# GpSimd's gain product one unit later behind the next reciprocal, and 64x64 blocks for half of the attention values

## The chip, the core and the metric

One core of a Trainium2 chip runs the whole program. The metric is the device time of one execution in microseconds (us); the time of a kernel is the median of its runs. The core has five engines with a queue of instructions each: PE (TensorE, matrix products; PEld is its loading of stationary operands), DVE (VectorE), ACT (ScalarE), POOL (GpSimd) and SP (SyncE, which here only issues transfers). Each engine works through its queue in order; engines wait for each other through semaphores. Transfers issued by SP and by POOL lie in separate queues and share 16 DMA engines.

## What is computed

```python
kv  = einsum('bhsd,bhse->bhde', k, v)            # 8 batches, 8 heads, 576 positions, 64 wide
o   = einsum('bhsd,bhde->bhse', q, kv)
x   = o / sqrt(mean(o*o, -1) + 1e-6) * g_norm    # then (batch*position, head*64): 4608 x 512
# mixture of experts on x
do  = x @ w_skip > 0
e   = argmax(x @ w_gate);  p = softmax(x @ w_gate)[e]
out = x;  out[do] += p * (relu(x @ w1[e]) @ w2[e])   # 8 experts, 512 -> 1024 -> 512
```

All data are fp32. There is no softmax in the attention, so that k^T v is formed once for each head, as a 64x64 matrix.

## The kernel before

**Two phases.** Up to about 130 us the attention runs, in 36 units; behind it the experts run one after the other (layers at lines 983, 994 and 1062). x is not kept on the chip: each finished piece is stored to `out`, and the experts gather their rows from there.

**Units.** A unit (`units`, line 390) is 256 positions of one batch (two rows for each of 128 partitions) and four of the eight heads (`u`). A batch b has four units with i = 0, 1; after batches 3 and 7 come two units with i = None, which hold the ninth part of the positions of four batches. Units 0 to 15 are batches 0 to 3, 16 and 17 the first i = None pair, 18 to 33 batches 4 to 7, 34 and 35 the last pair.

**Steps.** The order of all instructions is written out by hand (`tc.manual_schedule()`, line 138), in the loop at line 823. Step n issues:

1. PE: `turn(n+1)`, the transposes of q for the next unit (L421), copied out by ACT (L424);
2. ACT: `root(n-1)`, the square root (L486);
3. PE: `values(n)`, the products of q with k^T v (L457, or L465 where i is None) into one bank pair of PSUM; two such tiles (`o_ps`) take turns, and from unit 28 on (`THIRD`) every third unit uses `sum_ps` instead. ACT squares the result (L471);
4. DVE: `norm(n-1)`, reciprocal (L493) and the product xl = o times reciprocal (L496), which frees the PSUM tile;
5. DVE: `squares(n)`, the sum of squares (L479);
6. PE: the parts of k^T v for a later batch that fall in this step (`jobs(n, "pe")`): `state` three times (L350, in 64x64 blocks), `state_t` (L364), `state_m` (L373), `state_s` (L382), from six steps ahead of the batch's first unit;
7. POOL: `finish(n-1)`: sums of the gate logits lp and lg (L513, and for u = 1 also L517, L521), then the product of xl and g_norm into xb (L531), and after the last unit of a batch the store of half of xb (L552 or L546);
8. DVE: some two to four small operations of the expert choice ("gating"), if a group of units is complete: streams start at steps 12 and 22 (`ends`), and the last group is done after the attention (`choose(LAST)`, line 1310);
9. SP: `jobs(n, "end")`: loads of q, k and v (L115) and the other half of the store (L553 or L547), which is put at the end of step n+1.

In `values`, lines 456 to 461, a unit with a real i takes four products with 128x128 stationary q and 146 columns of a block-diagonal k^T v (two 64x64 heads and zeros beside them); a unit with i = None takes sixteen products of 64x64 blocks with 73 columns (lines 462 to 469), because its four quarters belong to four batches.

**Buffers.** xl has four buffers, xb (one for each batch) two, so the first product of batch b waits until both store halves of batch b-2 have landed. k and v have three buffers, q two.

**What follows the second gating stream.** Its DVE operations rank the experts (`rank_experts`, L667 to L705, steps 24 to 26). L695 writes the order of the experts; SP reads it (L709) and issues the two loads of the first expert's weights, 2 MB each (L309, L312), ahead of the SP half of batch 5's store. `early` (L742 to L763) then computes the first 128 rows, and POOL gathers them (L763).

**After the attention** PE transposes those rows (L960), does part of layer 1 (L983), then the rank of the last group (`rank(LAST)`, L596), the rest of layer 1, and from the row tables made on DVE (L720 to L729) POOL gathers the remaining rows (L950).

## Time and profile before

| | |
|---|---|
| median of 3 runs | 404.38 us (403.63 to 410.05) |
| the profiled execution | 406.39 us, span 404.6 us, mean granted PE clock 0.954 |
| busy share of the span | PE 91%, PEld 79%, DVE 63%, ACT 36%, POOL 31% |
| values L457, 128x128 by 146 | 240 records, mean 298 ns |
| product L531 | 32 (and 4 for i = None), mean 1199 ns |
| xl L496 / sum of squares L479 | 33 and 3, mean 767 ns / 36, mean 678 ns |
| first step / last xl / first transposes of expert rows | 20 us / 130.6 us / 129.4 us |

A line of a timeline has the start in us, the duration in us, the engine, the line of the code, the operation and its operands (what is written before the arrow, what is read after it), the shape and a count of merged records; in brackets the idle time ahead of it and what ended it. An fp32 product of PE has two records of each kind, so "x8" is four products and "x32" sixteen. In the chain of waits a line has start, duration, and what the program's end waited for in that time. In the windows table a row is a stretch with the busy time of each engine, the clock that PE was granted (1.00 is full), the share of the DMA engines in use and GB/s.

### The profile page before, as it was taken

The numbers are of one execution on the slowest core, as the hardware profiler recorded it, in microseconds if no ns is written. First come the engines' busy times: TensorE is split into PE (matmuls) and PEld (weight loads), VectorE is DVE, ScalarE is ACT, GpSimd is POOL, SyncE is SP. The second block draws the span as 40 slices with busy tenths as digits, with TensorE's granted clock in tenths as the row PEclk, the third lists the DMA queues.
The fourth block names the chain that finished last, engine by engine and source line by source line (L and its number), as shares of the span: only waits on it lengthen the run. The fifth ranks groups of instructions, "written<-read, shape, count | busy, mean of one in ns | idle before, by whom it ended". The sixth has DMA issues, their size and how long they took to land.

```text
span 404.6 us, 9627 instructions
## 1 busy us (share of the span) xinstructions
PE 369.5 (91%) x3849; PEld 320.9 (79%) x3849; DVE 253.8 (63%) x623; ACT 144.6 (36%) x384; POOL 125.0 (31%) x197
## 2 busy tenths in 40 slices
PE   6889999899964988999999999989989999999992
PEld 3678987788863948759978987968978988988982
DVE  3233568599977762457674665846765866868821
ACT  1365786566644212203401430520430340431410
POOL 7024576565567333113103302201231211112001
PEclk9589999899968899999999999989999999999998
DMA  8999999996595892427334551670752743710001
GB/s 297 394 390 389 336 363 375 291 346 182 158 396 159 234 365 75 156 106 231 108 160 129 205 211 58 227 256 3 259 194 80 259 146 119 259 54 27 28 2 48
DMA packets 31287, 81.70 MB, mean 202 GB/s; under 512 B 1850, under 2 KB 1858, under 8 KB 31236
## 3 DMA queue, kind: packets, MB, share of 16 engines
q1 hardware_dynamic: 26688, 66.59, 47.0%
q0 software_dynamic: 4528, 14.41, 10.9%
q8 instruction: 32, 0.52, 0.5%
q14 instruction: 19, 0.16, 0.1%
q10 hardware_dynamic: 20, 0.02, 0.0%
HBM read 66.80 MB, written 14.48 MB: 201 GB/s over the span
## 4 chain that ended last, share of the span: by engine, by line
PE 50%; DMA 17%; issue 15%; DVE 10%; POOL 3%; ACT 3%; DVEq 0%; POOLq 0%; ACTq 0%
PE bank L1062 22%; DMA out_dram<-xg,rows 7%; PE bank L994 7%; PE bank L983 5%; DMA out_dram<-xb 4%; PE o_ps L457 4%; DMA xg<-out_dram,src 3%; DVE xl L496 3%; PE sum_ps L350 3%; DMA xg<-out_dram,asrc 2%; PE q_ps L421 2%; PE bank L960 1%; DVE rs L479 1%; PE g_ps L364 1%; POOL out_dram L1204 1%
## 5 line engine op out<-in xcount | busy, mean ns | idle before, releaser
L1072 ACT COPY p<-bank 128x128 f32<-128x128 f32 (+6 forms) x70 | 20.8, 297 | 106.7 <-PE bank L1062 92.6
L1062 PE MATMUL bank<-xt,w 128*128 128x128 f32 (+5 forms) x336 | 55.4, 288 | 0.0
L1066 DVE TENSOR_TENSOR bank<-bank,p 128x128 f32<-128x128 f32 (+6 forms) x70 | 23.6, 337 | 41.6 <-PE bank L1062 40.7
L1062 PEld LDWEIGHTS bank<-xt,w 128*128 128x128 f32 x336 | 47.0, 190 | 1.9 <-DVE bank L1066 1.4
L457 PE MATMUL o_ps<-kvd,qT 128*128 128x146 f32 x240 | 37.0, 298 | 3.9 <-DVE xl L496 1.8
L1204 POOL DMA_INDIRECT out_dram<-xg,rows x16 | 16.2, 1012 | 76.2 <-DVE xg L1201 74.7
L531 POOL TENSOR_TENSOR xb<-xl,g_b 128x512 f32<-128x512 f32 x32 | 38.4, 1199 | 1.3 <-DMA out_dram<-xb 1.3
L457 PEld LDWEIGHTS o_ps<-kvd,qT 128*128 128x128 f32 x240 | 32.8, 195 | 5.8 <-DVE xl L496 3.0
L1062 PE MATMUL bank<-xs,s 128*128 128x128 f32 (+5 forms) x224 | 36.7, 289 | 0.0
L994 PE MATMUL bank<-w,ht 128*32 128x128 f32 (+2 forms) x448 | 36.6, 322 | 0.0
L1204 POOL DMA_INDIRECT out_dram<-xg,arows x8 | 9.0, 1130 | 81.0 <-DVE xg L1201 80.7
L950 POOL DMA_INDIRECT xg<-out_dram,src x15 | 16.2, 1082 | 53.4 <-DMA out_dram<-xg,rows 27.9
L479 DVE TENSOR_REDUCE rs<-sq 128x8 f32<-128x512 f32 x36 | 24.4, 678 | 12.4 <-ACT sq L471 12.2
L1062 PEld LDWEIGHTS bank<-xs,s 128*128 128x128 f32 x224 | 31.1, 190 | 1.0 <-ACT p L1072 0.8
L994 PEld LDWEIGHTS bank<-w,ht 128*32 128x32 f32 (+2 forms) x448 | 20.4, 121 | 13.6 <-issue 10.9
L1062 PE MATMUL bank<-w,ht 128*128 128x256 f32 x112 | 28.7, 401 | 0.1
L496 DVE TENSOR_TENSOR xl<-o_ps,rs 128x584 f32<-128x584 f32 x33 | 25.3, 767 | 4.0
L350 PE MATMUL sum_ps<-v,k 64*64 64x64 f32 x1152 | 25.6, 232 | 2.0 <-DMA v<-in_v_dram 1.8
L1062 PE MATMUL bank<-t,ht 128*128 128x256 f32 x112 | 27.1, 385 | 0.0
L350 PEld LDWEIGHTS sum_ps<-v,k 64*64 64x64 f32 x1152 | 22.4, 143 | 5.1 <-issue 3.1
L1062 PE MATMUL bank<-t,hs 128*128 128x256 f32 x112 | 25.6, 382 | 0.0
L513 POOL TENSOR_TENSOR lp<-xl 128x36 f32<-128x36 f32 x36 | 9.2, 256 | 52.1 <-DVE xl L496 50.5
(201 smaller groups left out, 708.5 us busy)
## 6 DMA issues: line engine op xcount, KB each, us to landing
w<-in_moe_w_dram SPq DMA_DIRECT2D x16, 2048.0 KB, 10.5
q<-in_q_dram SPq DMA_DIRECT2D x8, 1152.0 KB, 10.3
k<-in_k_dram SPq DMA_DIRECT2D x7, 1152.0 KB, 13.2
v<-in_v_dram SPq DMA_DIRECT2D x7, 1152.0 KB, 14.2
out_dram<-xb SPq DMA_DIRECT2D x8, 512.0 KB, 7.9
out_dram<-xb POOLq DMA_DIRECT2D x8, 512.0 KB, 6.9
k<-in_k_dram SPq DMA_DIRECT2D x2, 576.0 KB, 5.3
v<-in_v_dram SPq DMA_DIRECT2D x2, 576.0 KB, 6.3
```

The lines of the kernel that those rows point to most:

```text
L350: nc.tensor.matmul(out=sum_ps[w * 64:(w + 1) * 64, a, u, :], lhsT=kt[r, 2 * u + w, c, :], rhs=vt[r, 2 * u + w, c, :], start=(c == 0), stop ...
L457: nc.tensor.matmul(out=ps[:, w, 0:2 * PK].rearrange("p (r k) -> p r k", r=2)[:, :, cols], lhsT=qT[:, w, a, :], rhs=kvds[b % KVD][:, u, w, ...
L479: nc.vector.tensor_reduce(out=rs[:, :, :], in_=sq[:, :, :, :].rearrange("p x y (a d) -> p x (y a) d", a=2), axis=AX.X, op=ALU.add)
L496: nc.vector.tensor_tensor(out=xl[:, :, :, :].rearrange("p x y (a k) -> p x (y a) k", a=2), in0=ps[:, :, 0:2 * PK].rearrange("p x (h k) -> ...
L531: late.append(lambda: nc.gpsimd.tensor_tensor(out=xb[:, :, 4 * u * D:(4 * u + 4) * D].rearrange("p r (w x) -> p r w x", w=2), in0=xl[:, :, ...
L950: nc.gpsimd.indirect_dma_start(out=x_of(xg, off, m), out_offset=None, in_=cut_rows(m)[:, :], in_offset=bass.IndirectOffsetOnAxis(ap=idx[:, ...
L983: nc.tensor.matmul(out=hps[:, cols], lhsT=w_sb[r][0][:, dc, f * P:(f + 1) * P], rhs=xt[:, dc, cols], start=(dc == 0), stop=(dc == DC - 1))
L994: nc.tensor.matmul(out=yps[q * m:(q + 1) * m, 0:n], lhsT=ht[:, f, off:off + m], rhs=w_sb[r][1][:, f, q * n:(q + 1) * n], start=(f == 0), s ...
L1062: nc.tensor.matmul(out=out, lhsT=lhsT(i), rhs=rhs(i), start=start and i == 0, stop=i == k - 1, skip_group_check=True)
L1066: nc.vector.tensor_tensor(out=to, in0=x, in1=y, op=ALU.add)
L1072: nc.scalar.copy(out=t, in_=x)
L1204: ins = nc.gpsimd.indirect_dma_start(out=cut_rows(m)[:, :], out_offset=bass.IndirectOffsetOnAxis(ap=rows[:, col:col + 1], axis=0), in_=x, ...
```

## The change

Three things change in the attention loop.

**The product L531** of unit n is no longer issued right behind lp and lg of unit n. It is issued in `norm(n+1)`, ahead of that unit's lp on POOL, and gets a wait on the reciprocal of unit n+1. The last two products run at the end, as before. The stores follow: the POOL half directly behind the delayed product, the SP half at the end of step n+2 instead of n+1. On SP this puts the store halves up to batch 4's behind the load that they stood ahead of: one of q, or for batch 3's those of k and v of batch 7. On POOL the gather L763 now stands ahead of the product of unit 29 and of batch 6's store half, where it stood behind them.

**The values** of units 5, 9, 10, 11, 15, 19, 23 and 27 to 33 are computed by sixteen 64x64 blocks with 73 columns as in the i = None units, instead of four 128x128 products with 146 columns. These are the units from 5 on whose step holds no `state` part. The two halves in PSUM are then in the order of the i = None units, so the lp and xb reads use that order for these units too.

**The rest** moves helper code: `todo`, `at` and `jobs` are defined earlier, and the stores become two functions. Between the two orders, only the named instructions on POOL and SP differ in place; the order on PE, DVE and ACT is the same but for the values of these 14 units.

```diff
+    sums_at = {n - 6 + j for n, x in enumerate(units) if x[2:] == (0, 0) and x[1] for j in range(3)}
+    quarters = {n for n, x in enumerate(units) if x[2] is None or n >= 5 and n not in sums_at}
+
     late = []
+    WAIT = mybir.DependencyInfo(mybir.DependencyClass.Sync, mybir.DependencyReason.SCHED_ONLY)
...
-                if i is not None:
+                if n not in quarters:
                     nc.tensor.matmul(
                         out=ps[:, w, 0:2 * PK].rearrange("p (r k) -> p r k", r=2)[:, :, cols],
                         lhsT=qT[:, w, a, :], rhs=kvds[b % KVD][:, u, w, :, cols],
...
-                            lhsT=qT[rows, w, hf, a * 64:(a + 1) * 64],
-                            rhs=kvds[(4 * b + 2 * hf + r) % KVD][rows, u, w, r, cols],
+                            lhsT=qT[rows, w, a, to] if i is not None else
+                            qT[rows, w, hf, a * 64:(a + 1) * 64],
+                            rhs=kvds[(4 * b + 2 * hf + r if i is None else b) % KVD][rows, u, w, r, cols],
...
-        nc.vector.reciprocal(out=rs[:, :, :], in_=rs[:, :, :])
+        inverse = nc.vector.reciprocal(out=rs[:, :, :], in_=rs[:, :, :])
+        if n < NU - 1:
+            scale(n, inverse)
...
-        late.append(lambda: nc.gpsimd.tensor_tensor(
+        store = None
+        if u == 1 and i is None:
+            store = store_8
+        elif u == 1 and i == NQ - 1:
+            store = store_4
+        late.append((lambda: nc.gpsimd.tensor_tensor(
             out=xb[:, :, 4 * u * D:(4 * u + 4) * D].rearrange("p r (w x) -> p r w x", w=2),
-            in0=xl[:, :, :, G:G + 2 * D] if i is None else
+            in0=xl[:, :, :, G:G + 2 * D] if n in quarters else
             xl[:, :, :, G:G + 2 * D].rearrange("p w r x -> p r w x"),
             in1=g_b[:, :, :].rearrange("p a d -> p (a d)").unsqueeze(1).unsqueeze(1)
-                .to_broadcast([P, 2, 2, 2 * D]), op=ALU.mult))
-        if n == NU - 2:
-            return None
-        while late:
-            late.pop(0)()
...
+                .to_broadcast([P, 2, 2, 2 * D]), op=ALU.mult), store and (lambda: store(b))))
+        if n == NU - 1:
+            scale(NU)
+
+    def scale(n, behind=None):
+
+        while late:
+            job, store = late.pop(0)
+            ins = job()
+            if behind:
+                tc.add_manual_dep(ins.ins, behind.ins.name, WAIT, reason="VectorE's port is free then")
+            if store:
+                at(min(n + 2, NU + 1), "end", store())
...
-        store = done() if done else None
-        if store:
-            at(n + 1, "end", store)
+        if done:
+            done()
```

`store_8(b)` and `store_4(b)` issue the POOL half of the store and return the job that issues the SP half, with the same addresses as before.

More of the change, by code (lines that the diff above doesn't have):

```diff
@@ L405, with at, jobs @@
     assert GB + (TG + 1) * E <= 512
+    sums_at = {n - 6 + j for n, x in enumerate(units) if x[2:] == (0, 0) and x[1] for j in range(3)}
+    quarters = {n for n, x in enumerate(units) if x[2] is None or n >= 5 and n not in sums_at}
     late = []
+    todo = {}
+    WAIT = mybir.DependencyInfo(mybir.DependencyClass.Sync, mybir.DependencyReason.SCHED_ONLY)
+    def at(step, part, job):
+        todo.setdefault((step, part), []).append(job)
+    def jobs(step, part):
+        for job in todo.pop((step, part), []):
+            job()
     qTs, q8s, ops, rss, halves, lgs, xbs = {}, {}, {}, {}, {}, {}, {}
@@ L511, in finish @@
         lp = halves[nq]
-        pair = ends_of(xl[:, :, :, :])
+        pair = ends_of(xl[:, :, :, :] if n not in quarters else
+                       xl[:, :, :, :].rearrange("p r w k -> p w r k"))
         nc.gpsimd.tensor_tensor(out=lp[:, u, :, :, :], in0=pair[:, :, :, 0, :],
@@ L518, in finish @@
                                     in1=lp[:, 1, :, :, :], op=ALU.add)
-            both = lp[:, 0, :, :, :] if i is not None else \
-                lp[:, 0, :, :, :].rearrange("p r w g -> p w r g")
-            nc.gpsimd.tensor_tensor(out=lgs[g][:, t0:t0 + 2, :], in0=both[:, 0, :, :],
-                                    in1=both[:, 1, :, :], op=ALU.add)
+            nc.gpsimd.tensor_tensor(out=lgs[g][:, t0:t0 + 2, :], in0=lp[:, 0, 0, :, :],
+                                    in1=lp[:, 0, 1, :, :], op=ALU.add)
         if i is None:
@@ L534, in finish @@
             xl[:, :, :, G:G + 2 * D].rearrange("p w r x -> p r w x"),
             in1=g_b[:, :, :].rearrange("p a d -> p (a d)").unsqueeze(1).unsqueeze(1)
-                .to_broadcast([P, 2, 2, 2 * D]), op=ALU.mult))
-        if n == NU - 2:
-            return None
+                .to_broadcast([P, 2, 2, 2 * D]), op=ALU.mult), store and (lambda: store(b))))
+        if n == NU - 1:
+            scale(NU)
+    def scale(n, behind=None):
         while late:
-            late.pop(0)()
-        if u == 0:
-            return None
@@ L543, in finish @@
-        if i is None:
-            xb = xbs.pop((b, None))
-            rows = out.rearrange("(f hf r p c) d -> f hf p r c d", f=NF, hf=2, r=2, c=C)[b]
-            nc.gpsimd.dma_start(out=rows[0, :, :, C - 1, :], in_=xb[0:64, :, :])
-            return lambda: nc.sync.dma_start(out=rows[1, :, :, C - 1, :], in_=xb[64:128, :, :])
-        if i == NQ - 1:
-            xb = xbs.pop((b, 0))
-            rows = out[b * S:(b + 1) * S, :].rearrange("(p c) d -> p c d", c=C)[:, 0:4 * NQ, :]
-            rows = rows.rearrange("p (i hf r) d -> hf p i (r d)", hf=2, r=2)
-            nc.gpsimd.dma_start(out=rows[0], in_=xb[0:64, :, :, :].rearrange("p i r d -> p i (r d)"))
-            return lambda: nc.sync.dma_start(
-                out=rows[1], in_=xb[64:128, :, :, :].rearrange("p i r d -> p i (r d)"))
@@ L555, in finish, with store_8 @@
-        return None
+            job, store = late.pop(0)
[4 more added lines that the diff above has]
+                at(min(n + 2, NU + 1), "end", store())
+    def store_8(b):
+        xb = xbs.pop((b, None))
+        rows = out.rearrange("(f hf r p c) d -> f hf p r c d", f=NF, hf=2, r=2, c=C)[b]
+        nc.gpsimd.dma_start(out=rows[0, :, :, C - 1, :], in_=xb[0:64, :, :])
+        return lambda: nc.sync.dma_start(out=rows[1, :, :, C - 1, :], in_=xb[64:128, :, :])
@@ L558, with store_4 @@
+    def store_4(b):
+        xb = xbs.pop((b, 0))
+        rows = out[b * S:(b + 1) * S, :].rearrange("(p c) d -> p c d", c=C)[:, 0:4 * NQ, :]
+        rows = rows.rearrange("p (i hf r) d -> hf p i (r d)", hf=2, r=2)
+        nc.gpsimd.dma_start(out=rows[0], in_=xb[0:64, :, :, :].rearrange("p i r d -> p i (r d)"))
+        return lambda: nc.sync.dma_start(
+            out=rows[1], in_=xb[64:128, :, :, :].rearrange("p i r d -> p i (r d)"))
     ohbs, rks = {}, {}
@@ L777 @@
             in_=zero[:, :])
-    todo = {}
-    def at(step, part, job):
-        todo.setdefault((step, part), []).append(job)
-    def jobs(step, part):
-        for job in todo.pop((step, part), []):
-            job()
     starts = {}
```

## The prediction

> **What bounds the kernel now.** I read the busy tenths of the page first, since every edit lies in the attention. 40 slices of 10.1 us; the attention fills the first thirteen.

> ```profile
> PE   6889999899964988999999999989989999999992
> ...
> DVE  3233568599977762457674665846765866868821
> ...
> PEclk9589999899968899999999999989999999999998
> ```

> PE is nearly full up to slice 10, DVE from slice 7 to 11, and in slices 11 and 12 neither is. So the limit changes hands, and I went to the chain of waits (57 to 137 us), then to the timeline at each place where it changes.

> ```profile
> 98.13 1.18 DVE key L667
> 99.33 0.18 DVE key L673
> ...
> 101.51 0.98 DVE is_at L684
> ...
> 107.17 15.70 DMA out_dram<-xb
> 122.90 0.09 issue
> 123.00 1.19 POOL xb L531
> ...
> 131.46 5.58 PE bank L983 x33
> ```

> From 81 to 104 us the chain runs on DVE; then 15.7 us hang on one store, then on GpSimd's product of unit 30. L667 and L673 both write 8 numbers, and one takes seven times as long. The timeline says why (last two lines), and shows the two forms of the values:

> ```profile
> 60.62 1.17 PE L457 MATMUL o_ps<-kvd,qT 128*128 128x146 f32 x8
> ...
> 68.28 0.74 PE L465 MATMUL o_ps<-kvd,q 64*64 64x73 f32 x32
> ...
> 98.08 1.19 POOL L531 TENSOR_TENSOR xb<-xl,g_b 128x512 f32<-128x512 f32 x1
> 98.13 1.17 DVE L667 TENSOR_TENSOR key<-top,ebase 128x8 f32<-128x8 f32 x1
> ```

> L667 starts inside a product and ends with it (99.27, 99.30). SP's timeline shows the store of 107.17 queued behind 4 MB of weights, and the waits show who wants it:

> ```profile
> 106.09 0.40 SPq L309 DMA_DIRECT2D w<-in_moe_w_dram  x1
> 106.69 0.38 SPq L312 DMA_DIRECT2D w<-in_moe_w_dram  x1
> 107.17 22.97 SPq L553 DMA_DIRECT2D out_dram<-xb  x3
> ```

> ```profile
> POOL xb L531 <- DMA out_dram<-xb: 1.3, 1, 1.3
> ```

> [...] L667 is blocked, while xl (one input from PSUM) takes 0.77 us and the sum of squares 0.68 with or without a product beside them. [...] 32 records of 224 ns fill 0.74 us. [...] 0.50 was granted from 116 to 120 us, after an idle stretch of 2.6. [...]

> **The values, 14 units.** In PE's queue an L457 unit occupies 1.10 us (60.62 to the next L350 at 61.72), an L465 unit 0.67 (68.28 to 68.95); the chain has 1.00 and 0.67. I take 0.38 saved for each, between 0.15 (1.10 less the 0.95 that the L465 of 73.12 took at a clock of 0.81) and 0.43. ACT and DVE see the same number of instructions.

> **The product.** Removed from DVE are the waits for it. Against their unblocked kin (0.35 us for L631 from the last group, 0.17 to 0.25 for the others), the blocked ones lose: steps 12 to 17, L569 0.69, L574 0.86, L586 0.68, L625 0.56, in sum 2.8 us; 82 to 116 us, L631 1.17+0.10+0.91, L569 0.70, L582 0.82, L667 1.00, L684 0.83, L625 1.36, L631 1.07, L742 0.80, in sum 8.8. Behind the reciprocal the product (1.19) lies beside xl and the sum of squares (0.77+0.68 less overlap), which it doesn't block. Added: lp, L517 and L521 (0.26 each) now come after the product and meet the gating operations, and L566, which needs lg, starts 0.4 later at steps 12 and 22. I charge 0.1 to 0.2 a step for the former (a blocked L631 pair at 85.94 lost 0.10); at worst 0.26 for each of ten operations, 2.6.

> Queued behind the product's new wait on POOL are lp and lg of the next unit, the store and the gather. Two products, four small sums and their gaps take some 3.4 us for two units and a store 1.0 us for four, about 1.95 a unit, less than the 2.06 of the fastest steps (xl at 128.53 and 130.59). So POOL keeps up, with nothing to spare. xl's fourth buffer covers the later release. SP's stores: q and k, v for batch 7 are issued earlier or alike, and the stores have a batch's time to land; hidden by the DMA lull of 90 to 110 us (0.62 and 0.52 busy), else a store lands 3 us later (1.15 MB ahead of it at 390 GB/s). The gather is issued ahead of one product and one store, some 2.4 us earlier against its index; it isn't needed before 129 us, so nothing.

> **What of it reaches the weights' issue (106.09).** Up to step 11 PE is dense: units 5, 9, 11 give 3 x 0.38 = 1.1; unit 10's is lost in the wait for xl at 55.39. Steps 12 to 17: PE is dense but for 0.83 at 66.27, and the later L566 takes some: 0.7. Steps 18 to 25: unit 19 0.38; the wait of 0.29 at 85.48; step 23, which shrinks from 3.03 us to PE's own 2.26 (values 0.7, L364 0.96, transposes 0.6): in sum 1.4. The rest of DVE's saving there is hidden behind PE, which is 94 to 97% busy. At the end DVE is alone ahead of L695: L667 and L684 give 1.83, of which 0.4 meets inputs that aren't there yet: 1.4. Sum 1.1+0.7+1.4+1.4 = 4.6 us; weights at 101.5.

> **What the tail makes of it.** The store of batch 5 lands 16.8 us after the weights' issue (122.90-106.09), now at 118.3. DVE is further ahead: steps 26 to 35 need 10 x 2.06 plus about 2.9 of gating that the square root's 0.4 us gap doesn't hold, 23.5, against 27.2 (103.42 to 130.59); with unit 31 held up by a cold PE the last xl comes some 7.3 us earlier. So what is late next is POOL: product 30 waits for the store from about 114 on, and from its start to the last lg POOL is full (123.00 to 132.33, 9.3 us): lg at 127.7. The last choice takes 3.3 us more (132.33 to 135.61): 131.0. Before, PE came to the rank products at 137.55; with transposes 7.3 earlier it is there at 130.2, so the choice decides: 6.5 us gained.

> From here all moves together but the second expert's weights (135.50), which follow the last store on SP and come only 4.6 us earlier. The gather of 146.09 takes 6.07 us while these fill the DMA engines (1.02 and 1.06), and PE waits 2.2 us for it. Its landing comes between 4.6 and 6.5 earlier; I take 5.5. The experts behind it are unchanged. 406.39-5.5 = 400.9 for the profiled execution, which lies 2.0 above the median: **398.9 us**.

> **Rivals.** *All of it passes.* At 70.75 PE stands still for 1.33 us, and then runs 0.95 us longer at a clock of 0.81 (L350 1.50 instead of 0.86, L421 0.97 for 0.66). Without that stall the weights go 6.9 earlier, the choice ends at 128.7 and PE arrives at 127.9: 8.9 gained at the rank, and with the gather free of the weights 395.5 us. For it: the stall follows on a late L586, a blocked one; against: the page calls it "issue", no wait that it can name.

> *PE takes it.* If four-at-once blocks save nothing between 128-wide products, only DVE's lead at L667 and L684 (1.8) and PE's waits on xl (0.29, 0.59, 0.25) count: weights 3.0 earlier, 401.4 us. For it: PE is dense from 77 to 104 us. Against: the L465 of 68.28 stood between 128-wide products too. It also covers products that come late behind a store's 0.65+0.3 us on POOL and block DVE again, that is, a change that does half of what it says.

> *Slower: PE's own queue.* Sixteen small products are 24 records of each kind more a unit, 336 in all. PE stands still for "issue" ahead of L350, whose blocks are as small: 3.3 us in 7 gaps over 24 parts, 0.14 a part, but the gap of 70.75 was 1.33. If each of the seven changed units ahead of the weights drew such a gap, 9.3 us would be lost against 4.6 gained: about 409 us. It decides from 0.66 us a unit on. Against: none of the four L465 units shows one.

> **How the numbers follow.** Forecast 0.49 (396.5 to 401.5 alone), all passes 0.22, PE takes it 0.23, slower 0.06. 394.0 to 404.0 leaves out the last and half of the second case's faster side. 2% is 8.1 us, about what a measurement of this kernel can tell from no change: faster means under 396.3, most of the second case and the first one's edge, 0.22; slower means over 412.5, 0.03; within, 0.75.

> **What would show it.** Right: L667, L684, L625, L742 at 0.17 to 0.25 us; changed values at 0.75; weights issued near 101.5; product 30 waiting about 4 us for the store; PE waiting up to 1 us ahead of L596. Wrong: gating operations still about 1 us long, weights issued after 104, PE gaps within the blocks, or a landing of batch 5's store that doesn't follow the weights.

## The result, and the profile after

The changed kernel takes 404.73 us in the median (402.17 to 409.91, 22 runs) beside 405.31 for the kernel before (400.15 to 411.71, 22 runs). Eleven of before's runs and one of the changed kernel's lie over 1.5% above the fastest of their kernel, as does before's profiled execution (406.39), and count as slow ones; the ratio of the others, on which everything below rests, is 1.0059, with a 95% interval of 1.0036 to 1.0083, while the medians of all runs point the other way (0.9986). The forecast was 398.9, a gain of 1.4%. By neither count is that gain there; by the first 0.6% was lost, within the 2% either way. The profiled execution took 405.63 us, and its span is 0.7 us shorter than before's (403.9 and 404.6).

The busy tenths of the page after, in slices of 10.1 us:

```profile
PE   7889998889775969999999999989999999999992
...
DVE  2333668477685960466674774856866866868821
...
PEclk8599999899996996999999999999999999999998
```

DVE has less to do in slices 8 to 11, as forecast. But PE, which was at 9 in slice 11 (101 to 111 us), is at 7 there, and PEclk shows a 6 in slice 16, where before it had full speed. The first is explained by the chain of waits, here from 85 us on:

```profile
88.83 0.72 PE sum_ps L350 x35
89.55 1.40 issue
90.95 0.45 PE sum_ps L350 x13
...
102.65 1.91 issue
104.56 0.49 PE sum_ps L350 x14
...
106.96 1.20 POOL xb L550
108.18 13.82 DMA out_dram<-xb
...
122.16 1.18 POOL xb L550
```

Where before's chain ran on DVE, it now runs on PE and breaks off in the middle of a group of small products: 35 of 48, then nothing for 1.40 us, then 13. "issue" means that nothing shown held PE back; such a standstill is called a break from here on. Further breaks end at 71.78 us (1.93), 111.36 (1.16) and 118.11 (0.84), the last two inside the new blocks: 7.2 us in five, beside 1.3 us in one before. The edits themselves did what they should (PE's, DVE's and SP's timelines after):

```profile
92.13 0.74 PE L477 MATMUL o_ps<-kvd,qT 64*64 64x73 f32 x32
```
```profile
97.87 0.17 DVE L693 TENSOR_TENSOR key<-top,ebase 128x8 f32<-128x8 f32 x1
```
```profile
104.05 0.40 SPq L309 DMA_DIRECT2D w<-in_moe_w_dram  x1
104.64 0.38 SPq L312 DMA_DIRECT2D w<-in_moe_w_dram  x1
108.18 21.11 SPq L580 DMA_DIRECT2D out_dram<-xb  x3
```

A changed unit takes 0.74 us instead of 1.17, L693 (L667 of before) 0.17 instead of 1.17. The weights go at 104.05 (before 106.09, forecast 101.5), the store behind them only 4.1 us later, since its product waited for a reciprocal behind the break of 102.65. The second surprise is behind the choice, in PE's timeline (before, then after):

```profile
152.21 0.98 PE L960 MATMUL bank<-ident,xg 128*128 128x128 f32 x7 [2.20 <-DMA xg<-out_dram,src]
153.99 6.00 PE L983 MATMUL bank<-xt,w 128*128 128x212 f32 x32 [0.79 <-ACT xt L965]
```
```profile
149.69 0.66 PE L976 MATMUL bank<-ident,xg 128*128 128x128 f32 x4 [2.90 <-DMA xg<-out_dram,src]
150.84 0.90 PE L976 MATMUL bank<-ident,xg 128*128 128x128 f32 x3 [0.49 <-DMA xg<-out_dram,asrc]
152.09 8.92 PE L999 MATMUL bank<-xt,w 128*128 128x212 f32 x32 [0.35 <-ACT xt L981]
```

The gather lands 2.5 us earlier, and then the same 32 products take 8.92 us instead of 6.00. The windows table after has PE's granted clock in the column behind POOL: 0.50.

```profile
152.00:155.00 3.00, 2.91 (x8) 2.77 (x9) 0.00 (x0) 0.04 (x1) 0.94 (x1) 0.50 0.30 87
155.00:158.00 3.00, 3.00 (x10) 2.81 (x10) 0.00 (x0) 0.35 (x1) 0.00 (x0) 0.50 0.00 0
```

### The profile page after: what moved, and what is told of

The parts are those of the page before. It is cut to its first block, busy times and chain, and to the rows that moved or that the text cites. A ratio compares the mean times of both kernels' runs of the same rounds, so it can differ in the third digit from the quotient of the medians.

```text
span 403.9 us, 10297 instructions
## 1 busy us (share of the span) xinstructions
PE 366.3 (91%) x4185; PEld 315.0 (78%) x4185; DVE 244.1 (60%) x623; ACT 144.4 (36%) x384; POOL 124.8 (31%) x197
## 4 chain that ended last, share of the span: by engine, by line
PE 60%; DMA 14%; issue 12%; DVE 6%; POOL 4%; ACT 2%; ACTq 0%; POOLq 0%; DVEq 0%
PE bank L1078 29%; PE bank L1010 7%; DMA out_dram<-xg,rows 6%; PE sum_ps L350 4%; PE o_ps L469 4%; PE bank L999 4%; DMA out_dram<-xb 3%; PE q_ps L433 3%; DMA xg<-out_dram,asrc 2%; PE g_ps L364 2%; DMA xg<-out_dram,src 2%; POOL xb L550 2%; PE bank L976 2%; PE o_ps L477 1%; DMA xb<-in_g_norm_dram 1%
## 5 line engine op out<-in xcount | busy, mean ns | idle before, releaser
L1078 PEld LDWEIGHTS bank<-xt,w 128*128 128x128 f32 x336 | 47.0, 190 | 2.4 <-DVE bank L1082 1.9
L350 PE MATMUL sum_ps<-v,k 64*64 64x64 f32 x1152 | 26.8, 236 | 4.4 <-issue 3.6
L350 PEld LDWEIGHTS sum_ps<-v,k 64*64 64x64 f32 x1152 | 23.2, 146 | 7.6 <-issue 5.6
L1078 PE MATMUL bank<-w,ht 128*128 128x256 f32 x112 | 27.2, 386 | 0.0
L999 PE MATMUL bank<-xt,w 128*128 128x128 f32 (+1 forms) x128 | 23.9, 354 | 1.3 <-ACT xt L979 1.0
L999 PEld LDWEIGHTS bank<-xt,w 128*128 128x128 f32 x128 | 22.6, 225 | 2.3 <-ACT xt L979 1.3
L1078 PEld LDWEIGHTS bank<-t,ht 128*128 128x128 f32 x112 | 20.8, 190 | 4.1 <-issue 1.6
```

What stands on the lines that cost most here:

```text
L350: nc.tensor.matmul(out=sum_ps[w * 64:(w + 1) * 64, a, u, :], lhsT=kt[r, 2 * u + w, c, :], rhs=vt[r, 2 * u + w, c, :], start=(c == 0), stop ...
L999: nc.tensor.matmul(out=hps[:, cols], lhsT=w_sb[r][0][:, dc, f * P:(f + 1) * P], rhs=xt[:, dc, cols], start=(dc == 0), stop=(dc == DC - 1))
L1078: nc.tensor.matmul(out=out, lhsT=lhsT(i), rhs=rhs(i), start=start and i == 0, stop=i == k - 1, skip_group_check=True)
```

## Theories

**A, supply of instructions.** The page's list of queues has a row that I had passed over (after):

```profile
q8 instruction: 35, 0.57, 0.6%
```

**C, the rival**: an unnamed wait that belongs to these instructions or their data. **B**: the breaks come from the product's new place or from DVE being ahead.

**E**: what the rank gained is lost to the half clock behind the wait for the gather. **D**: only what comes behind the choice sets the time.

## Experiments

**x1_product: the product alone.**

```diff
-    quarters = {n for n, x in enumerate(units) if x[2] is None or n >= 5 and n not in sums_at}
+    quarters = {n for n, x in enumerate(units) if x[2] is None}
```

> The product one unit later, and all values in the form they had before (the changed units take 8 wide products again). Theory A (PE's instructions come in blocks of 256 records of 64 bytes; a fetch takes some 2.3 us from its packet, and a run of 64x64 products uses up what is left of the block in less): with 24 records less in each of 14 units the only standstill for issue over 0.6 us stays the one near 70 us, as before; the standstills of 89.6, 102.7, 110 and 117 us are gone. The weights go at 102 to 103.5 us (before 106.09, changed kernel 104.05), the span is 1 to 4 us shorter than before's. Theory B (the standstills come from the product's new place, or from DVE running ahead): they stay, some 5 us in sum, and the time is that of the changed kernel.

Ratio to before 0.9955 (0.9915 to 0.9995), weights at 104.17, span 399.2. The breaks of 102, 110 and 117 us are gone. (A unit has 48 records less, 24 of each kind.) I missed two things: one break moved rather than went (91.75 us, 1.45), and that near 70 us grew to 1.96; the weights went 0.7 us later than expected. This speaks for A against B, as to most of the breaks; the product's edit alone gains.

**x2_blocks: the blocks alone** (the edit to `quarters` and the three places that use it, in the kernel before).

> The 64x64 blocks in the 14 units alone; product, store and their order as before. Theory A: the standstills for issue come back at the same PE record numbers as in the changed kernel, within some records of 2498, 3266, 3778, 4035, 4291, and cost 5 to 6 us in sum; the blocks save 0.36 us each on PE, about 3 us of it on the path, so the time is 0 to 3 us longer than before's and 1 to 4 us longer than that of the product alone. Theory B: no more standstills than before (1.3 us), and a time some 1 to 3 us below before's.

Ratio 1.0136 (1.0073 to 1.0198): 5.5 us lost. PE's timeline:

```profile
63.18 0.27 PE L443 MATMUL o_ps<-ident,q 128*128 128x128 f32 x1 [2.81 <-issue]
69.53 0.60 PE L468 MATMUL o_ps<-kvd,qT 64*64 64x73 f32 x21 [1.12 <-issue]
75.79 0.43 PE L607 MATMUL g_ps<-ohb,ones 128*128 128x8 bf16 x10 [2.03 <-issue]
110.33 0.46 PE L350 MATMUL sum_ps<-v,k 64*64 64x64 f32 x14 [2.54 <-issue]
```

Four breaks, 8.5 us, at records 1986, 2242, 2498 and 3778: 194 + a multiple of 256 again, but only two of the five expected places. The loss is larger than I expected (0 to 3 us), and B falls: the product and its order are before's here. The two edits together (1.0059) come to about the product of each alone, 0.9955 x 1.0136 = 1.009.

**x3_shift: the changed kernel, 128 records more in front.**

```diff
-    for _ in range(9):
+    for _ in range(2):
...
+    for _ in range(71):
+        nc.tensor.matmul(out=warm_ps[:, 0:1], lhsT=ones[:, :], rhs=ones[:, 0:1], start=True,
+                         stop=True)
```

> The changed kernel with 64 more small products (128 records) in front: of the nine wide warm-up products seven are left out and 71 of one column put in. Nothing else differs. Theory A: a standstill stays at PE records 191 + a multiple of 256, so it hits other instructions: the ones that stood at the changed kernel's records 2370, 2626, 3138, 3394, 3650, 3906, 4162, and those of 89.6, 102.7, 110.2 and 117.3 us are gone. How many there are, and so the time, depends on what is dense there: 3 us either way. Theory C (a wait that the profile doesn't name, tied to these instructions or to their data): the standstills stay at the same instructions, whatever runs in front.

Ratio 1.0007 (0.9963 to 1.0052). The breaks at 111 and 117 us inside the blocks and those in L350 at 89.6 and 102.7 are gone, others came; by records they lie where A has them (191 in the expectation is 194 by the count used since). The list of all programs but x9 (breaks over 0.55 us from 40 us to the last values, without PE's waits for DVE's tables):

```
before             2242
changed            2498 3266 3778 4034 4290
x1_product         2242 3010
x2_blocks          1986 2242 2498 3778
x3_shift           1730 2498 2754 3010 4546
x5_store_first     2498 3266 3778 4290
x6, x8, x11        2242 3010
x7_warm_gather     2498 2754 3266 3778      (changed kernel's attention)
x10_warm_wait      2242 2498 3010 3778      (changed kernel's attention)
x12_before_shift   2498 2754 3522
x13_all_blocks     2498 3266 3778 4290
```

Every number is 194 + a multiple of 256. Which of them turn into breaks differs even between executions of one and the same attention.

**x12_before_shift: the kernel before, with the same 128 records in front.**

> The kernel before with 128 more PE records in front, put in as in x3. Theory A: the boundary near 70 us moves off the rank products and the standstill of 1.33 us there is gone; standstills appear where before's records 2114, 2370, 2626, 2882, 3138, 3394 fall in runs of small or four-byte 128-wide products that last under 2.3 us, one to four of 0.5 to 2 us; the time moves by -1 to +4 us with not one instruction of the attention changed. Theory C: the standstill stays at the rank products of step 14, no other appears.

Ratio 1.0108 (1.0068 to 1.0148), 4.4 us, just over the top of what I expected:

```profile
74.40 0.91 PE L353 MATMUL sum_ps<-v,k 64*64 64x64 f32 x42 [1.80 <-issue]
83.89 0.69 PE L424 MATMUL q_ps<-ident,q 128*128 128x128 f32 x2 [3.04 <-issue]
108.75 0.81 PE L353 MATMUL sum_ps<-v,k 64*64 64x64 f32 x38 [1.82 <-issue]
```

Not one instruction of the attention differs from before, yet 6.7 us of breaks stand where 1.3 did, and the one at the rank products is gone. C falls. The changed front itself costs nothing: from 37 to 80 us this execution is 0.3 to 1.3 us ahead of before's. At 94 us it is 4.2 us behind; between the two lie the break of 3.04 us and half clock from 83.2 to 90.0 us, which sets in before the break is over. So a break can cost more than its own length. And the kernel before, as given, lies well: by the two places of the boundaries that were tried it takes 1 and 1.0108, the changed kernel 1.0059 and 1.0007 (these two aren't apart).

**x9_dense: the supply by itself.** 512 products of 64x64 by 64x73 on data that nobody reads, in front of before's attention; one run.

> The kernel before with 512 products of 64x64 by 64x73 (2048 PE records, data that nobody reads) put in front of the attention, to measure the supply alone. Theory A: PE stands still once every 256 records, with one 16 KB packet of instructions ahead of each; without standstills 256 records take 2.7 us at full clock; with them one period is 4 to 5 us, 8 periods 32 to 40 us in all. Theory C (the standstills belong to the attention's instructions or data): 2048 records run through in about 21 us, no standstill over 0.5 us.

```profile
5.02 3.98 PE L200 MATMUL o_ps<-ident 64*64 64x73 f32 x214
12.88 3.73 PE L200 MATMUL o_ps<-ident 64*64 64x73 f32 x128 [3.87 <-issue]
19.07 3.90 PE L200 MATMUL o_ps<-ident 64*64 64x73 f32 x128 [2.46 <-issue]
25.27 3.32 PE L200 MATMUL o_ps<-ident 64*64 64x73 f32 x128 [2.30 <-issue]
29.00 2.55 PE L200 MATMUL o_ps<-ident 64*64 64x73 f32 x128 [0.41 <-issue]
32.45 2.26 PE L200 MATMUL o_ps<-ident 64*64 64x73 f32 x128 [0.91 <-issue]
36.45 2.26 PE L200 MATMUL o_ps<-ident 64*64 64x73 f32 x128 [1.75 <-issue]
```

128 records of products and as many of weight loads are 256. PE stops after every 256, and goes on 2.36 to 2.45 us after a packet's start; the page has 40 packets, eight more, for 2048 records more. The whole lasts from 5.0 to 40.8 us, 35.8, in the range of A, but by luck: the four groups from 12.88 us on took 4.5 us longer than the 2.26 us of the later ones, with half clock behind each of the first three breaks, which A didn't count. What I hadn't expected either: the break isn't constant. In the first three the packet starts only when the block is used up, and 2.3 us and more are lost; later it starts 59 to 163 records ahead, and 0.4 to 1.75 us are lost.

**x5_store_first: the weights behind batch 5's store.**

```diff
-        return lambda: nc.sync.dma_start(
-            out=rows[1], in_=xb[64:128, :, :, :].rearrange("p i r d -> p i (r d)"))
+
+        def send():
+            nc.sync.dma_start(
+                out=rows[1], in_=xb[64:128, :, :, :].rearrange("p i r d -> p i (r d)"))
+            if b == 5:
+                load_weights(0, wpool_a)
+
+        return send
...
-            load_weights(0, wpool_a)
+            pass
```

> The changed kernel with the first expert's 4 MB of weights issued on SP behind batch 5's store instead of ahead of it. Theory A (the store's landing is behind the weights, and product 30 waits for it): the store lands within 4 us of its issue (108.2 to 112 instead of 122.07), product 30 starts at 120.8 instead of 122.16 as its xl is there, the last lg comes 1.4 us earlier at 129.3, and the rank products of 134.07 up to 1.4 us earlier; the weights land near 126, ahead of their first use at 127.9 or up to 1 us late for it. Span 0 to 1.4 us shorter than the changed kernel's. Theory D (what comes after the choice sets the time, the gather and the clock of PE above all): the rank comes earlier, the span doesn't change by more than 0.5 us.

Ratio 1.0017 (0.9981 to 1.0053), which isn't apart from the changed kernel's. GpSimd's wait for stores fell from 2.6 to 0.6 us, the last lg came at 129.03 (1.5 earlier), as expected. But the rank products started at 135.31, 1.2 us later: PE's clock was half from 119.8 to 133.4, and the 40 products ahead of the rank took 7.1 us instead of 6.07; the break at 118.6 had grown to 2.44. With POOL's wait gone, PE is late next. Neither theory had that: both had the rank earlier. The span is 2.2 us shorter all the same, which speaks against D as far as one execution can.

**x6_product_store: x1 with x5's edit.**

> The product one unit later with the old values, and the first expert's weights behind batch 5's store on SP. Theory A: product 30 loses its wait for the store (x1: last lg at 130.13, its rank products at 133.67); lg comes 1 to 2.5 us earlier, but PE, at half clock from 120 to 133 us, needs until 132.5 to 133.5 for the first expert's products ahead of the rank, so 0 to 1 us reaches the end: ratio to before 0.993 to 0.996 (x1 0.9955). Theory D (only what comes after the choice counts): the same time as x1, 0.9955.

Ratio 0.9891 (0.9841 to 0.9942, 6 runs), better than expected, though the interval reaches into what A expected. The rank at 131.97 is 1.7 us ahead of x1, and the second expert's weights, which follow the last store on SP, go at 129.43 instead of 133.47, so the gather lands 2.4 us earlier. Its wait (1.99 us) still brings half clock from 147.2 to 154.0.

**x7_warm_gather: twelve wide products of ones ahead of a gather's transposes, a misplaced test.**

> The changed kernel with twelve wide bf16 products of ones that nobody reads, put in PE's queue ahead of the transposes that wait for the gather of the second expert's rows (146.8 to 149.7 us in the changed kernel). Theory E (the gain at the rank, 3.5 us, is lost again because the wait there lowers PE's clock to half for 6.8 us): PE's clock stays at 1.0 from 135 to 160 us, the 32 products of 128x212 behind take 6.0 to 6.3 us instead of 8.9, the span is 2 to 3.4 us below the changed kernel's, ratio to before 0.997 to 1.001. Rival: the half clock there costs nothing in the end because the next experts wait for their weights or gathers; ratio as the changed kernel's, 1.004 to 1.008.

Ratio 1.0096 (1.0057 to 1.0135). PE's timeline says why:

```profile
168.93 2.75 PE L1271 MATMUL bank<-ones 128*128 128x512 bf16 x12
```

They ran at 168.93, ahead of the next expert's transposes, where PE had no wait; half clock stood from 149.8 to 156.7, as in the changed kernel. It tells nothing of E; at most it says that useless work in a full PE doesn't help (1.0096 against 1.0059, with intervals that overlap).

**x10_warm_wait: the same twelve in the right place.**

```diff
+        warm = bank()
+        for _ in range(12):
+            nc.tensor.matmul(out=warm[:, :], lhsT=ones[:, :],
+                             rhs=ones[:, :].unsqueeze(1).to_broadcast([P, 4, P]),
+                             start=True, stop=True)
         for piece in plan[0]:
             expert_in(xg0, xt0, piece)
```

> The changed kernel with twelve wide bf16 products of ones directly ahead of the transposes that wait for the first gather behind the choice (in x7 they stood one gather later, behind the 212-wide products, where PE had no wait: 2.75 us added). Theory E: PE works through the wait of 2.9 us, its clock stays at 1.0 from 131 to 160 us, the 32 products of 128x212 take 6.0 to 6.3 us instead of 8.9, the span is 2 to 3.4 us below the changed kernel's, ratio to before 0.997 to 1.001. Rival (the half clock there is hidden by what comes after, or follows on something else than the wait): ratio 1.004 to 1.008, or a half clock there all the same.

Ratio 0.9971 (0.9943 to 0.9999), apart from the changed kernel's 1.0059.

```profile
148.05 2.75 PE L1346 MATMUL bank<-ones 128*128 128x512 bf16 x12
151.05 0.66 PE L976 MATMUL bank<-ident,xg 128*128 128x128 f32 x4 [0.25 <-DMA xg<-out_dram,src]
151.99 0.55 PE L976 MATMUL bank<-ident,xg 128*128 128x128 f32 x3 [0.28 <-DMA xg<-out_dram,asrc]
153.05 6.00 PE L999 MATMUL bank<-xt,w 128*128 128x212 f32 x32 [0.52 <-ACT xt L981]
```

The work fills the wait, the 32 products are back at 6.00, and although this execution came to them 1 us later than the changed kernel, its span is 2.1 us shorter. E stands.

**x8_product_store_warm: x6, x7's misplaced products, and twelve more behind the last values.**

> Candidate: product one unit later, old values, weights behind batch 5's store, twelve wide products of ones ahead of the gather's transposes and twelve behind the last values (where PE waits from about 122 to 126 us and its clock falls to half). Theories A and E together: rank products near 131.5, full clock from 130 to 160 us, ratio to before 0.985 to 0.992. Rival (each gain is hidden by the next wait, the gather's landing behind the second expert's weights): not below x1's 0.9955.

Ratio 0.9968 (0.9938 to 0.9997), missed. The ones behind the last values worked: full clock from 76 to 144 us, rank at 129.38 (x6 131.97). But the other twelve again added 2.75 us where PE was full (163.61), and half clock stood from 144.2 to 151.1.

**x11_product_store_warm2: x8 with the second set, now of nine, in the right place.**

> x6 (product one unit later, old values, weights behind batch 5's store) with ten or more wide products of ones behind the last values, as in x8, and nine directly ahead of the transposes that wait for the first gather behind the choice. Theory E: rank products near 129.5 as in x8 (x6 131.97), full clock from there to 160 us, the 32 products of 128x212 at 6.0 to 6.3 us (x6 8.9); 3 to 5 us less than x6, ratio to before 0.977 to 0.985. Rival: what the warm clock gives is lost in the waits for the gathers and weights behind it, 0.987 to 0.991 as x6.

Ratio 0.9843 (0.9795 to 0.9891): 6.3 us faster than before and the lowest here, with 6 runs and an interval that overlaps x6's. Rank at 129.44, the 32 products at 6.00, and the clock full from 74.7 us to 388.7.

**x13_all_blocks: x11 with the blocks.**

> x11 with the 64x64 blocks in the 14 units again, so that they are weighed where no half clock stands behind them (x11 0.9843, half clock only from 71 to 75 us). Theory A (the blocks cost through the supply of instructions, by themselves): standstills at PE records 194 + a multiple of 256, 4 to 6 us more of them than x11's 2.8 us, batch 5's store issued 1.5 to 3 us later than x11's 104.97; ratio to before 0.989 to 0.996. Rival (the blocks cost only because they upset what follows, the clock above all): 0.980 to 0.986, as x11 or below.

Ratio 0.9967 (0.9941 to 0.9993), just above the range of A and far above the rival's. Four breaks, 7.7 us (x11: 2.8), and the weights, right behind batch 5's store, at 109.44 (x11 105.81), which is more than expected. Half clock came back too, from 152.0 to 155.5 (the 32 products 7.49 us), so up to 1.5 us of the 5.0 us is not the supply itself.

## Why the prediction was wrong

By its own steps, in the profiled executions:

- **The edits' direct effects: right.** Values 0.74 against 0.75 us; L667, L684, L625 and L742 of before at 0.17 to 0.25. xl and the sum of squares, beside which the product now lies (product from 93.34 us, xl from 93.36, the sum from 94.04), keep their means of 0.77 and 0.68 us. The port that the diff's `reason` names was not shown; these times were. Two operations near 65 us stayed blocked (L608 0.94 and L612 0.58 us): the product beside the first had waited 1.23 us for a store, and the one beside the second came right behind it.
- **The weights' issue: wrong by 2.55 us** (104.05 for 101.5). The sum of gains has no term for PE's supply. The break of 71.78 is 0.6 longer than before's, that of 89.55 is new with 1.40: 2.0 of the 2.55. (The clock of 0.81 that the prediction reads near 73 us is 3.4 us of half clock behind before's break; the changed kernel has the same from 72.7 us.)
- **The store "lands 16.8 us after the weights' issue": 18.0.** The break of 102.65 delayed the reciprocal that product 25 waits for, and with it the store. It landed at 122.07, 0.8 earlier than before; 4.6 were forecast. Product 30 waited 1.37 us for it, not 4, since the breaks of 111 and 118 us had made its own input late. They cost the rank little: in x1, which has neither, product 30 stood still for 3.07 us, and the rank came only 0.4 us earlier than in the changed kernel (133.67).
- **POOL and choice behind it: right** (last lg 8.6 us after product 30's start, 9.3 forecast; 3.3 us of choice, as forecast). Rank 3.6 us earlier instead of 6.5, gather landed 2.5 earlier instead of 5.5.
- **"The experts behind it are unchanged": wrong.** The 32 products took 2.92 us longer at half clock. At 160 us the changed kernel was 1.0 us behind, and PE's work stays 1.0 us behind before's at every place up to 262 us. Then before's own execution falls back by 1.4 us, where it waits 1.32 us for a gather and has half clock from 268.1 to 271.5, and by 0.8 more at a wait of 1.70 (300.56). x12, whose code is the same there, gains 4.1 us on it in that stretch. So the spans of the two profiled executions, with the changed kernel 0.7 us ahead, don't show what the edits did.

The step that failed is the sum 1.1 + 0.7 + 1.4 + 1.4 = 4.6 us: it puts PE's supply of instructions at nothing. Instead the breaks rose from 1.3 to 7.2 us, the weights left 2.55 us later than forecast, and the rank gained 3.6 us, not 6.5. The second wrong step is that of the unchanged experts: they lost 2.9 us at half clock. The prediction has the supply only in its rival "Slower: PE's own queue", at 0.06. There the mechanism was the right one, and the 336 more records of each kind were counted; the size was not. I spread the breaks over units and asked whether a unit of small products draws one. The measured unit is the block of 256 records: each break lies at the end of one and is over 2.2 to 2.6 us after a packet's start (2.7 once). 256 records of dense small products are through in about that time (2.26 us in x9), where 256 of wide ones would last some 17.6 us (an estimate from 1.10 us for 16), so a packet is late for the small ones more easily. That none of four L465 units showed one said little, with a boundary every 256 records. The 16 KB packets were on the page of before, and so was one break of 1.33 us, which one of my rivals put down to a late DVE operation.

The blocks' own loss can't be given as one number: alone they cost 1.36%, on top of x11 1.26%, but the boundaries' place moves with them, and moving it alone cost before 1.08%. That the supply makes the breaks is shown by x3, x9 and x12, and that the half clock behind the gather cost about what the rank had gained by x10 (0.9971 beside 1.0059); what makes a packet start early or late is open.

## What to carry to other kernels

Splitting products into smaller ones adds records even where it saves time (here 48 a unit, for 0.74 us instead of 1.17): number PE's records, see where 256-record boundaries fall in dense stretches, and count with breaks of 0.6 to 3.0 us there, as in the attentions here, and with half clock at some of them (in the changed kernel behind the 1.93 us, not behind the 1.91); an edit anywhere in front moves them all, so compare two kernels at more than one offset before a difference under 1% is put down to the edit. Follow a gain to the next wait of PE and look at the clock behind it: twelve useless wide products in a wait of 2.9 us gave back 0.9% here (x10). Compare two traces at a place behind the edit as well as at their ends, for a wait elsewhere can outweigh the edit. An edit in two parts is tried in parts: here one part gained 0.4% and the other lost 1.4%.

## What the runs showed of the hardware

Half clock came in stretches of one to four times 3.41 us that start on one grid: in the changed kernel at 72.7, 123.9 and 151.2 us, the latter two 15.0 and 23.0 times 3.413 us after the first; they last 3.41, 6.83 and 6.83 us, and one ahead of the attention, from 7.9 us on, lasts 13.65. Waits of 1.99 and 0.65 us (x6) brought 6.8 us of half clock, while before's 2.20 and 0.79 brought none, so the length of the wait alone doesn't decide.

I added up PE's idle time in each window of the grid, from 50 to 380 us in all 14 traces, and took those at full clock. Half clock followed none of the windows with less than 1.19 us idle, all 19 with more than 2.01 us, and 25 of the 55 between. The two waits of before lie in two windows (2.01 and 0.99 us), the changed kernel's 2.90 us puts 2.37 into one. What decides between 1.19 and 2.01 us is open; the ends of products are modelled in these traces.
